# Attention with mixture-of-experts: raw w2 requested at the end of a step, and new w2 split ahead of scaling y and joining h

## The chip, the cores and the metric

The kernel runs on one core of one Trainium2 chip. The metric is the device time of one launch in microseconds (us). Engines are named as in the profile: PE (TensorE, matmuls), PEld (its weight loads), DVE (VectorE), ACT (ScalarE), POOL (GpSimd) and SP (SyncE), which issues DMAs. "SPq" and the like are the instruction queues of an engine.

## What is computed

A chunked attention is followed by a mixture of experts on its output.

```python
def reference(q, k, v, w_gate, w_local, w1, w2):   # q, k, v: (8, 8, 576, 64)
    # attention inside chunks of 64 tokens, per batch and head
    scores = (q_c @ k_c^T) / sqrt(64); attn = softmax(scores); out = attn @ v_c
    x = out.transpose(0, 2, 1, 3).reshape(8, 576, 512)
    # one expert per token: argmax of x @ w_gate, or the expert of the token before
    # where sigmoid(x @ w_local) >= 0.5
    h = relu(x[b, s] @ w1[e])                      # w1: (8, 512, 1024)
    out[b, s] = softmax(x @ w_gate)[e] * (h @ w2[e])   # w2: (8, 1024, 512)
```

There are 4608 tokens, 8 experts, and everything is float32.

## The kernel before

The attention comes first and writes x to DRAM. The tokens are then sorted by expert into tiles of at most 128 tokens, and the experts' part works on one tile after another. The change lies in this second part, in `step(t)` (lines 1053 to 1127), which runs for t = 3 to 40 here.

A matmul in full float32 is slow on PE, so the weights and the activations of a full tile are split into a rounded high part and the rest (hi and lo): `split` (line 104) makes `w2h` on ACT (line 105) and `w2l` on DVE (line 106) from `raw2`, in four chunks of 128x1024. One product is then three matmuls (hi hi, hi lo, lo hi). Every expert's remainder tile with at most 64 tokens is put first of its expert; such a *partial* tile is multiplied by the raw weights in plain float32 (`mm1_part`, line 664, and `mm2_part`, line 677, whose matmul is line 681), since the new weights aren't split yet. `kind[t]` says at run time whether tile t is partial, and every such choice is an If on registers.

Step t does, in program order:

- `mm1` of tile t (x times w1, into PSUM `h`), its softmax factor (`probs`, lines 644 to 651), and `planes` (line 723): ACT and DVE copy h into 16-bit planes `hw`.
- POOL gathers the rows of tile t + 2 from DRAM; PE transposes x of tile t + 1 (line 763) and ACT and DVE split it (`xp`, lines 751 and 752). `refill(0, t)` splits new w1 where the expert turns after tile t.
- SP issues two DMA transposes `ht<-hw` (`turn_planes`, line 730), if tile t is full.
- SP issues `reload(1, t - 2)`: raw w2 of the next expert, two loads of 1 MB, if `fetch[t - 2]` is set (lines 1025 to 1031; line 1027 is the If). Then `reload(0, t)`, the same for raw w1.
- PE multiplies h of tile t - 1 by w2 into PSUM `y`: `mm2` (line 674) or `mm2_part`.
- `down_y`: DVE scales y into `ysb` (line 816, or lines 707 to 710 for a partial tile), and POOL scatters ysb to the output (line 819).
- `h_parts`: for a full tile `join` (line 732) waits for ht, copies the turned halves into `hsb` (lines 736 and 737) and makes hi and lo of `hp` (lines 739 and 740). For a partial tile PE transposes hsb (line 780) and ACT and DVE copy it to `hf`.
- `refill(1, t - 1)`: ACT and DVE split new w2 where the expert turns after tile t - 1 (`turn[t - 1]`).

Each engine executes its own instructions in this order (a manual schedule); only semaphores tie the engines together. Steps from 36 on (`tail`) are written otherwise: there `refill(1, t - 1)` and `reload(1, t - 1)` already stand at the end. `y` and the two banks of `h` have one PSUM buffer each. SP's queue carries all weight loads and all transposes of h.

In the run profiled, the tiles 6, 9, 18, 21, 28 and 35 are partial, each the first of its expert; tile 27 is a full tile and the only one of its expert.

Of the kernel before, what the change touches and what calls it, by code (L numbers as in the profile page):

```python
# [33 lines left out]
EARLY = 3  # L34
NTILE = EARLY + (N + E * (P - 1)) // P
# [34 lines left out]
def tile_attention_then_moe(ctx: ExitStack, tc, q, k_in, v, wg, wl, w1, w2, out):  # L70
# [33 lines left out]
    def split(hi, lo, raw, lo_eng=None):  # L104
        nc.scalar.copy(hi, raw)
        (lo_eng or nc.vector).tensor_tensor(lo, raw, hi.bitcast(F32), ALU.subtract)
# [424 lines left out]
    for b in range(B):  # L531
        t, p = divmod(b * S, P)
# [99 lines left out]
    def probs(xg, hot):  # L632
        pr, atoms = prob_atoms(xg, hot)
        run(atoms[:-1])
        return pr, atoms[-1]
# [21 lines left out]
    def mm1(xs, hs, c):  # L657
        for n, (a, w) in enumerate(PASSES):
            for j in range(2):
                nc.tensor.matmul(hs[j], xs[a][:, c], W1[w][c][:, 512 * j:512 * j + 512],  # L660
                                 start=(c == 0 and n == 0), stop=(c == 3 and n == 2))


    def mm1_part(xf, hs, M):
        n = F * M // P
        for c in range(4):
            for j in range(P // M):
                nc.tensor.matmul(hs[0][M * j:M * j + M, 0:n], xf[:, c, 0:M], raw1[c][:, n * j:n * j + n],
                                 start=(c == 0), stop=(c == 3))
# [14 lines left out]
    def new_h():  # L684
        return [ps_s.tile([P, 512], F32, name=f"h{j}", tag=f"sc{j}") for j in range(2)], pc.tile([P, F + 32], F32, name="hsb", bufs=1)[:, 0:F]
# [4 lines left out]
    def either(kind, plain, partial, sizes=False):  # L690
        if kind is None:
            plain()
            return
        with tc.If(kind != 0) as cmp:  # L694
            if sizes:
                with tc.If(kind != 1) as small:
                    partial(P // 4)
                with small.Else():
                    partial(HT)
            else:  # L700
                partial()
        with cmp.Else():
            plain()
# [8 lines left out]
    def relu(hsb, hs):  # L712
        for j in range(2):
            nc.scalar.activation(hsb[:, 512 * j:512 * j + 512], hs[j], AF.Relu)

    def relu_part(hsb, hs, M):
        nc.scalar.activation(hsb[:, 0:F * M // P], hs[0][:, 0:F * M // P], AF.Relu)

    def new_planes():
        return (pa2.tile([P, 2, 2, 512], U16, name="hw", tag="xT", bufs=1),  # L720
                pa2.tile([P, 2, 2, 4, P], U16, name="ht", tag="pr"))

    def planes(hw, hs):
        for n in range(2):
            for j, eng in enumerate((nc.scalar, V)):
                evac(eng, hw[:, j, n], hs[j].bitcast(U16)[:, n::2])

    def turn_planes(hw, ht):
        for j in range(2):
            nc.sync.dma_start(ht[:, j].rearrange("p a n t -> p (a n) t"), hw[:, j].rearrange("p a f -> p (a f)"), transpose=True)  # L730
# [28 lines left out]
    def x_parts(xg, kind, late=False, own=False):  # L759
        xp = part("xp", "pT" if late else None)  # L760
        ps = trp().rearrange("p (n t) -> p n t", n=4)
        for n in range(4):
            nc.tensor.transpose(ps[:, n], xg[:, P * n:P * n + P], ident)
        xf = pc.tile([P, 4, HT], F32, name="xf", **own_tag("xf", own))
        either(kind and kind[1], lambda: split4(ps, xp), lambda: share(xf, ps[:, :, 0:HT]))
        return xp[:, 0], xp[:, 1], xf
# [167 lines left out]
    def gather_full(t):  # L934
        xgs[t] = gather(t, pc.tile([P, XR], F32, name="xg", bufs=4), x_d)
# [63 lines left out]
    def reg(row, t, hi, engines, why=None):  # L999
        return nc.values_load(regs[0:1, row, t:t + 1], min_val=0, max_val=hi, engines=engines,  # L1000
                              skip_runtime_bounds_check_because=why)
# [4 lines left out]
    def refill(which, t):  # L1006
        hi, lo, raw = ((w1h, w1l, raw1), (w2h, w2l, raw2))[which]
        with tc.If(turn[t] != 0):  # L1008
            for c in range(3 if which == 0 else 4):
                split(hi[c], lo[c], raw[c])  # L1010
            if which == 0:
                with when(kind[t + 1] and kind[t + 1][1] == 0):
                    split(hi[3], lo[3], raw[3])
# [11 lines left out]
    def reload(which, t):  # L1025
        dst, w, k = ((pair1, w1, 2 * P), (pair2, w2, 4 * P))[which]
        with tc.If(fetch[t] != 0):  # L1027
            en = reg(1, t + 1, E - 1, [ET.SP])
            for g in range(2):
                nc.sync.dma_start(  # L1030
                    dst[g], w[bass.ds(en, 1), k * g:k * g + k, :].rearrange("a (c p) f -> p (a c) f", p=P))

    TMIN = N // P
# [6 lines left out]
    @contextmanager  # L1040
    def when(v, otherwise=None):
        if v is None:
            yield
        else:
            with tc.If(v) as cmp:  # L1045
                yield
            if otherwise:
                with cmp.Else():
                    otherwise()
# [3 lines left out]
    def step(t):  # L1053
        tail = t >= TMIN
        if t < NTILE:
            hs, hsb = new_h()
            with when(ok[t]):
                either(kind[t] and kind[t][2], lambda: [mm1(xps[t], hs, c) for c in range(4)],
                       lambda M: mm1_part(xps[t][2], hs, M), True)
                prc[t], last = probs(xgs[t], ehot[:, t])  # L1060
                hw, ht = (None, None) if tail else new_planes()
                either(kind[t] and kind[t][1], lambda: (last(), relu(hsb, hs) if tail else planes(hw, hs)),
                       lambda M: (last(), relu_part(hsb, hs, M), split(w1h[3], w1l[3], raw1[3])), True)
                if tail and t + 1 < NTILE:
                    xps[t + 1] = x_parts(xgs[t + 1], kind[t + 1], t != LAST, t == LAST)
        if t + 2 < NTILE:
            with when(ok[t + 1]):
                gather_full(t + 2)
        if t + 1 < NTILE:
            next_x(t + 1)  # L1070
        if not tail:
            if kind[t] is None:
                turn_planes(hw, ht)
            else:
                with tc.If(kind[t][3] == 0):
                    turn_planes(hw, ht)
        if EARLY < t <= TMIN:
            reload(1, t - 2)
        if t + 1 < NTILE:
            reload(0, t)  # L1080
        if t + 2 < NTILE and t + 2 not in kind:
            kind[t + 2] = kind_of(t + 2)
        if t + 2 < NTILE:
            turns(t + 1)
        y = new_y()

        def down(cs):
            def plain():
                for c in cs:
                    mm2(hps[t - 1], y, c)  # L1090

            either(kind[t - 1] and kind[t - 1][2], plain,
                   lambda: mm2_part(hps[t - 1][0][2], y, range(2 * cs[0], 2 * cs[-1] + 2)))

        def down_y():
            keep = t == LAST
            ysb = new_ysb(t > LAST)
            with when(ok[t - 1], (lambda: V.memset(ysb, 0.0)) if keep else None):
                scale_y(ysb, y, prc[t - 1], kind[t - 1])
                if not keep:  # L1100
                    put_y(t - 1, ysb)
            if keep:
                kept.append((t - 1, ysb))

        if t < NTILE:
            hps[t], hp, hf = new_hp(tail and t != LAST, t == LAST)
        if tail and t < NTILE:
            cuts = ((0, 1, 2, 3),) if t == LAST else ((0, 1), (2, 3))
            with when(ok[t - 1]):
                down(cuts[0])  # L1110
            if t != LAST:
                with when(ok[t]):
                    h_parts(hsb, (0,), kind[t], hp, hf)
                with when(ok[t - 1]):
                    down(cuts[1])
            down_y()
            with when(ok[t]):
                h_parts(hsb, (1,) if t != LAST else (0, 1), kind[t], hp, hf)
            refill(1, t - 1)
            reload(1, t - 1)  # L1120
        else:
            with when(ok[t - 1]):
                down((0, 1, 2, 3))
            down_y()
            if t < NTILE:
                h_parts(hsb, (0, 1), kind[t], hp, hf, ht)
                refill(1, t - 1)

    def next_x(t):
        if EARLY < t <= TMIN:  # L1130
            xps[t] = x_parts(xgs[t], kind[t], t == TMIN)
        refill(0, t - 1)
# [44 lines left out]
```

## Time and profile before

| | us |
|---|---|
| median of two runs | 702.25 (700.42 to 704.07) |
| the profiled execution | 705.32 |
| its span, first to last instruction | 703.40 |
| PE busy in it | 622.7 |

The profile is of one execution of its own, and its times add up to 705.32, not to the median. A line of a timeline gives the start (us from the span's start), the duration, the engine, the source line, the operation, what it writes and reads, how many instructions were merged, and in brackets the idle time ahead of it and what ended that. The granted clock is a share of TensorE's full 2.4 GHz.

### The profile page before, as it was taken

What the parts mean: (1) busy time and instruction counts of PE and PEld (TensorE: products, weight loads), DVE (VectorE), ACT (ScalarE), POOL (GpSimd) and SP (SyncE); (2) the same over time, 40 slices, a digit from 0 to 9 for tenths busy, and PEclk for the clock granted to TensorE, in tenths of its full rate; (3) what the DMA queues carried; (4) which work ended last, traced back from release to release, by engine and by line L of the source; (5) the groups of instructions that cost most, each with busy time, mean ns of one, the idle gap of its engine ahead of it and who ended that gap; (6) DMA issues with size and microseconds to landing.
All of it is one profiled execution on the core that took longest, in us unless ns stands there. A gap on an engine that the chain in (4) does not pass through costs nothing. (4 is left out here: it accounts for less than half of the span.)

```text
span 703.4 us, 16455 instructions
## 1 busy us (share of the span) xinstructions
PE 622.7 (89%) x5458; PEld 487.4 (69%) x5458; DVE 408.2 (58%) x1008; ACT 308.8 (44%) x528; POOL 170.1 (24%) x286
## 2 busy tenths in 40 slices
PE   3899989779999968969999969889998699999993
PEld 3688867567778756648787646667876487877882
DVE  1566658675885775655555656744578445674331
ACT  2577756654313543523434444523456233453220
POOL 3334433672231211211212111212113112121101
PEclk9999999999999998989999989989999899999997
DMA  8999999987544443837554353629377385554201
GB/s 189 245 211 281 250 264 252 274 255 267 161 136 77 78 179 68 261 88 207 97 101 87 79 178 85 265 64 217 90 199 251 84 214 102 81 187 150 64 18 36
DMA packets 142318, 112.41 MB, mean 160 GB/s; under 512 B 99280, under 2 KB 118736, under 8 KB 142160
## 3 DMA queue, kind: packets, MB, share of 16 engines
q1 hardware_dynamic: 135520, 89.86, 51.7%
q0 software_dynamic: 6640, 20.65, 8.7%
q8 instruction: 75, 1.23, 0.7%
q14 instruction: 83, 0.68, 0.3%
HBM read 77.28 MB, written 20.35 MB: 139 GB/s over the span
## 5 line engine op out<-in xcount | busy, mean ns | idle before, releaser
L674 PE MATMUL y<-w2h,hp 128*128 128x512 f32 x560 | 186.3, 402 | 4.8 <-ACTq L1008 2.2
L660 PE MATMUL h<-w1h,xp 128*128 128x512 f32 x560 | 161.9, 398 | 0.0
L819 POOL DMA_INDIRECT out<-ysb,sidx x41 | 44.4, 1084 | 397.5 <-DVE ysb L816 274.1
L674 PEld LDWEIGHTS y<-w2h,hp 128*128 128x128 f32 x560 | 106.6, 190 | 27.5 <-ACTq L1008 2.7
L660 PEld LDWEIGHTS h<-w1h,xp 128*128 128x128 f32 x560 | 102.1, 188 | 20.0
L674 PE MATMUL y<-w2l,hp 128*128 128x512 f32 x280 | 110.9, 396 | 1.7 <-DVEq L1008 1.0
L660 PE MATMUL h<-w1l,xp 128*128 128x512 f32 x280 | 86.9, 391 | 0.0
L736 ACT COPY hsb<-ht 128x512 uint16<-128x512 uint16 x54 | 40.7, 772 | 92.3 <-DMA ht<-hw 86.7
L816 DVE TENSOR_SCALAR ysb<-y,ppr 128x512 f32<-128x512 f32 x35 | 26.3, 751 | 80.1 <-PE tr L802 45.1
L674 PEld LDWEIGHTS y<-w2l,hp 128*128 128x128 f32 x280 | 53.6, 191 | 13.5 <-DVEq L1008 2.2
L681 PE MATMUL y<-raw,hf 128*64 128x256 f32 x192 | 32.5, 510 | 33.9 <-SPq L1027 19.3
L660 PEld LDWEIGHTS h<-w1l,xp 128*128 128x128 f32 x280 | 52.5, 188 | 11.9 <-DVEq L1008 0.2
L179 PE MATMUL tr<-ident,qk 128*128 128x128 f32 x288 | 44.0, 301 | 14.1 <-POOL qk L171 6.4
L171 POOL COPY qk<-qk 128x512 f32<-128x512 f32 x69 | 40.1, 614 | 58.7 <-issue 26.3
L169 ACT COPY qkT<-tr 128x512 f32<-128x512 f32 x69 | 37.7, 589 | 30.1 <-PE tr L179 23.5
L681 PEld LDWEIGHTS y<-raw,hf 128*64 128x64 f32 x192 | 19.5, 188 | 45.2 <-issue 42.7
L179 PEld LDWEIGHTS tr<-ident,qk 128*128 128x128 f32 x288 | 34.9, 153 | 21.3 <-POOL qk L171 11.1
L739 ACT ACTIVATE hp<-hsb 128x512 fp32r<-128x512 f32 x54 | 31.0, 622 | 41.8 <-DVE hsb L737 40.0
L627 POOL DMA_INDIRECT xg<-x_d,gidx x39 | 44.6, 1143 | 15.1 <-issue 13.9
L646 ACT ACTIVATE pex<-pex 128x8 f32<-128x8 f32 x41 | 8.6, 210 | 84.3 <-DVE pex L645 84.3
L740 DVE SCALAR_TENSOR_TENSOR hp<-hsb,hp 128x512 fp32r<-128x512 f32 x54 | 35.0, 690 | 14.5 <-ACT hp L739 14.5
L171 DVE COPY hw<-h 128x512 uint16<-128x512 uint16 x54 | 34.8, 686 | 8.9 <-PE h L660 4.7
(220 smaller groups left out, 876.8 us busy)
## 6 DMA issues: line engine op xcount, KB each, us to landing
raw<-in_moe_w SPq DMA_DIRECT2D x28, 1024.0 KB, 6.5
raw<-in_moe_w SPq DMA_DIRECT2D x16, 512.0 KB, 5.6
qk<-in_q SPq DMA_DIRECT2D x11, 512.0 KB, 6.5
qk<-in_k SPq DMA_DIRECT2D x11, 512.0 KB, 7.0
v<-in_v SPq DMA_DIRECT2D x22, 256.0 KB, 6.0
x_d<-xs SPq DMA_DIRECT2D x7, 521.0 KB, 6.6
x_d<-x_w2h SPq DMA_DIRECT2D x6, 521.0 KB, 7.0
x_d<-x_w2l SPq DMA_DIRECT2D x5, 521.0 KB, 8.0
```

The lines of the kernel that those rows point to most:

```text
L169: eng.copy(dst, src)
L171: eng.tensor_copy(dst, src)
L179: nc.tensor.transpose(box["ps"][:, n], src_of(n), ident)
L627: nc.gpsimd.indirect_dma_start(out=dst, out_offset=None, in_=src, in_offset=bass.IndirectOffsetOnAxis(ap=gidx[t].bitcast(U32), axis=0))
L660: nc.tensor.matmul(hs[j], xs[a][:, c], W1[w][c][:, 512 * j:512 * j + 512], start=(c == 0 and n == 0), stop=(c == 3 and n == 2))
L674: nc.tensor.matmul(y, hx[f // 4][a][:, f % 4], W2[w][c][:, f % 2, :], start=(f == 0 and n == 0), stop=(f == 7 and n == 2))
L681: nc.tensor.matmul(y[HT * j:HT * j + HT, 0:n], hf[:, f % 4, HT * (f // 4):HT * (f // 4) + HT], raw2[f // 2][:, f % 2, n * j:n * j + n], st ...
L736: nc.scalar.copy(bits[:, j, :, :, 1], ht[:, j, 1])
L739: nc.scalar.activation(hp[j][:, 0], full[:, j], AF.Relu)
L740: V.scalar_tensor_tensor(hp[j][:, 1], full[:, j], 0.0, hp[j][:, 0].bitcast(F32), ALU.max, ALU.subtract)
L816: either(kind and kind[1], lambda: V.tensor_scalar(ysb, y, pr, None, ALU.mult), lambda: y_part(ysb, y, pr))
L819: nc.gpsimd.indirect_dma_start(out=out, out_offset=bass.IndirectOffsetOnAxis(ap=sidx[t].bitcast(U32), axis=0), in_=ysb, in_offset=None, bo ...
```

## The change

In steps below 36, raw w2 is no longer requested behind the transposes of step t for tile t - 2, but at the end of step t for tile t - 1, behind the w1 reload. And `refill(1, t - 1)`, the split of new w2, moves from the end of the step to right behind `mm2` of tile t - 1, ahead of the scaling of y and of `h_parts`.

```diff
@@ step(t)
                 with tc.If(kind[t][3] == 0):
                     turn_planes(hw, ht)
-        if EARLY < t <= TMIN:
-            reload(1, t - 2)
         if t + 1 < NTILE:
             reload(0, t)
...
         else:
             with when(ok[t - 1]):
                 down((0, 1, 2, 3))
+            if t < NTILE:
+                refill(1, t - 1)
             down_y()
             if t < NTILE:
                 h_parts(hsb, (0, 1), kind[t], hp, hf, ht)
-                refill(1, t - 1)
+                reload(1, t - 1)
```

SP's queue in step 5 before, from its transposes to the If of the w1 reload (raw_0_85 and raw_1_86 are raw w2, raw_0_83 and raw_1_84 raw w1, L1027 the If of a reload):

```order
L730 DMA_TRANSPOSE ht<-hw 128x8x128 x2
L1075 UNCONDITIONAL_BRANCH x2
L1027 COMPARE_AND_BRANCH
L1000 TENSOR_LOAD regs
L1000 ISA x2
L1030 ISA
L1030 DMA raw_0_85<-in_moe_w 128x4x512
L1030 ISA
L1030 DMA raw_1_86<-in_moe_w 128x4x512
L1027 UNCONDITIONAL_BRANCH x2
L694 UNCONDITIONAL_BRANCH
L1027 COMPARE_AND_BRANCH
```

In the changed kernel the transposes of step 5 are followed by the w1 reload at once; this is the end of that reload and what stands behind it, up to the branch at the end of the w2 reload:

```order
L1030 DMA raw_1_84<-in_moe_w 128x2x1024
L1027 UNCONDITIONAL_BRANCH x2
L1008 UNCONDITIONAL_BRANCH
L1000 TENSOR_LOAD regs x2
L1027 COMPARE_AND_BRANCH
L1000 TENSOR_LOAD regs
L1000 ISA x2
L1030 ISA
L1030 DMA raw_0_85<-in_moe_w 128x4x512
L1030 ISA
L1030 DMA raw_1_86<-in_moe_w 128x4x512
L1027 UNCONDITIONAL_BRANCH x2
```

The w2 reload has moved behind the w1 reload, and so out of the stretch between one step's transposes and the w2 matmuls of the same step. It stands ahead of the next step's transposes.

ACT's queue in step 5 before, from the join to the split of w2 (in brackets the semaphores that a row waits on: an engine's name, or DMAHW for the DMAs of SP):

```order
L736 COPY hsb<-ht 128x512 [waits DMAHW4_49,Activation_49]
L736 COPY hsb<-ht 128x512 [waits DMAHW5_49]
L739 ACTIVATE hp_4110<-hsb 128x512 [waits DVE_49,PE_49,Activation_49]
L739 ACTIVATE hp_4111<-hsb 128x512 [waits DVE_49,PE_49,Activation_49]
L694 UNCONDITIONAL_BRANCH
L1008 COMPARE_AND_BRANCH
L105 CAST w2h<-raw_0_85 128x1024 [waits DMAHW6_49,DMAHW3_49,Activation_49]
L105 CAST w2h<-raw_0_85 128x1024 [waits DMAHW7_49,Activation_49]
L105 CAST w2h<-raw_1_86 128x1024 [waits DMAHW7_49,DMAHW2_49,Activation_49]
L105 CAST w2h<-raw_1_86 128x1024 [waits DMAHW3_49,Activation_49]
```

The same place in the changed kernel, from the register loads at the head of the stretch to the first copy of hf:

```order
L1000 TENSOR_LOAD regs x2
L1008 COMPARE_AND_BRANCH
L105 CAST w2h<-raw_0_85 128x1024 [waits DMAHW4_49,DMAHW3_49,PE_49]
L105 CAST w2h<-raw_0_85 128x1024 [waits DMAHW7_49,PE_49]
L105 CAST w2h<-raw_1_86 128x1024 [waits DMAHW5_49,DMAHW2_49,PE_49]
L105 CAST w2h<-raw_1_86 128x1024 [waits DMAHW3_49,PE_49]
L1008 UNCONDITIONAL_BRANCH
L1008 UNCONDITIONAL_BRANCH [waits Activation_49]
L1027 UNCONDITIONAL_BRANCH
L694 COMPARE_AND_BRANCH
L696 COMPARE_AND_BRANCH
L169 COPY hf<-tr 128x2x2x32 [waits PE_49]
```

The four casts now stand ahead of hf and of the join, and each has a wait on PE of its own. On DVE the four subtractions (line 106) moved in the same way, ahead of the scaling of y.

PE's queue in step 5 before, at the w2 matmuls of a partial tile (line 681):

```order
L763 MATMUL tr<-ident,xg 128x128 x3
L694 UNCONDITIONAL_BRANCH x2
L1008 UNCONDITIONAL_BRANCH
L1075 UNCONDITIONAL_BRANCH
L1027 UNCONDITIONAL_BRANCH
L1000 TENSOR_LOAD regs
L694 COMPARE_AND_BRANCH
L681 MATMUL y<-raw_0_85,hf 64x256 [waits DMAHW4_49,DMAHW3_49,DMAHW6_49,DVE_49,Activation_49]
```

And in the changed kernel:

```order
L763 MATMUL tr<-ident,xg 128x128 [waits DMASW1_49]
L763 MATMUL tr<-ident,xg 128x128 x3
L1000 TENSOR_LOAD regs
L694 COMPARE_AND_BRANCH
L681 MATMUL y<-raw_0_85,hf 64x256 [waits DMAHW2_49,DMAHW3_49,DVE_49,DMAHW4_49,Activation_49]
```

The matmuls themselves don't move. They wait on DMA counters of SP in both; which counters these are has changed with SP's order.

## Rows read from the trace of the kernel before

**Rows 1.** Page, part 1: busy time, share, instructions of the engines

```profile
PE 622.7 (89%) x5458; PEld 487.4 (69%) x5458; DVE 408.2 (58%) x1008; ACT 308.8 (44%) x528; POOL 170.1 (24%) x286
```

**Rows 2.** Page, part 5: group, busy, mean ns | idle before, releaser

```profile
L681 PE MATMUL y<-raw,hf 128*64 128x256 f32 x192 | 32.5, 510 | 33.9 <-SPq L1027 19.3
```

**Rows 3.** Timeline of PE: line 681 at places 1 to 5, then the control

```profile
266.48 5.18 PE L681 MATMUL y<-raw,hf 128*64 128x256 f32 x32 [8.16 <-DMA ht<-hw]
...
306.49 5.64 PE L681 MATMUL y<-raw,hf 128*64 128x256 f32 x32 [6.86 <-SPq L1027]
...
418.55 5.93 PE L681 MATMUL y<-raw,hf 128*64 128x256 f32 x32 [6.46 <-DMA ht<-hw]
...
459.78 5.80 PE L681 MATMUL y<-raw,hf 128*64 128x256 f32 x32 [5.84 <-SPq L1027]
...
551.43 6.05 PE L681 MATMUL y<-raw,hf 128*64 128x256 f32 x32 [6.56 <-SPq L1027]
...
632.13 1.95 PE L681 MATMUL y<-raw,hf 128*64 128x256 f32 x16
```

**Rows 4.** Stretches: us; PE, PEld, DVE, ACT, POOL busy (count); clock, DMA, GB/s

```profile
258.00:266.50 8.50, 0.34 (x5) 0.14 (x3) 6.09 (x13) 3.04 (x6) 0.00 (x0) 0.78 0.67 193
266.50:272.00 5.50, 5.50 (x34) 3.50 (x35) 0.79 (x2) 1.53 (x2) 0.00 (x0) 0.72 0.14 31
...
634.00:637.00 3.00, 3.00 (x27) 2.00 (x26) 1.54 (x3) 1.26 (x3) 0.00 (x0) 1.00 0.05 11
```

**Rows 5.** Timeline of all engines around place 1 (tile 6 partial)

```profile
252.78 1.25 SPq L1030 DMA_DIRECT2D raw<-in_moe_w  x2
254.02 0.75 DVE L816 TENSOR_SCALAR ysb<-y,ppr 128x512 f32<-128x512 f32 x1 [1.52 <-issue]
...
255.31 0.29 DVE L171 COPY hf<-tr 128x128 f32<-128x128 f32 x1 [0.33 <-ACT hf L169]
255.37 3.89 ACT L105 CAST w2h<-raw 128x1024 fp32r<-128x1024 f32 x4
...
256.46 4.63 DVE L106 TENSOR_TENSOR w2l<-raw,w2h 128x1024 fp32r<-128x1024 f32 x4 [0.86 <-ACT w2h L105]
...
263.02 2.66 SPq L730 DMA_TRANSPOSE ht<-hw  x2
264.05 0.68 DVE L752 TENSOR_TENSOR xp<-tr,xp 128x512 fp32r<-128x512 f32 x1
```

**Rows 6.** Timeline of DVE and PE at place 5's turn (tile 27 full)

```profile
521.86 3.49 DVE L106 TENSOR_TENSOR w1l<-raw,w1h 128x1024 fp32r<-128x1024 f32 x3
526.76 0.75 DVE L816 TENSOR_SCALAR ysb<-y,ppr 128x512 f32<-128x512 f32 x1 [1.40 <-PE h L668]
...
528.65 1.29 DVE L740 SCALAR_TENSOR_TENSOR hp<-hsb,hp 128x512 fp32r<-128x512 f32 x2 [0.44 <-ACT hp L739]
...
530.13 0.49 PE L674 MATMUL y<-w2h,hp 128*128 128x512 f32 x1 [1.40 <-ACT w2h L105]
...
538.34 0.60 PE L780 MATMUL tr<-ident,hsb 128*128 128x128 f32 x4
```

**Rows 7.** SP: w2 load, next transposes; landings of both, and transposes without load (278.60)

```profile
323.38 1.19 SPq L1030 DMA_DIRECT2D raw<-in_moe_w  x2
330.84 4.54 SPq L730 DMA_TRANSPOSE ht<-hw  x2
...
DMA to landing us min/median/max: 5.6/8.6/11.6
...
DMA to landing us min/median/max: 5.2/5.5/5.8
...
DMA to landing us min/median/max: 3.1/3.1/3.2
```

**Rows 8.** Timeline behind place 1: join of tile 8, then its w2 matmuls

```profile
283.20 1.38 ACT L736 COPY hsb<-ht 128x512 uint16<-128x512 uint16 x2 [1.61 <-issue]
...
287.12 0.50 PE L674 MATMUL y<-w2h,hp 128*128 128x512 f32 x1
```

## Prediction, made before the changed kernel was run

> **What bounds the kernel now.** I read the page first, then TensorE's waits and timeline, then the stretches with their granted clock, and last all engines around one stall. PE is busy for 89% of the span [rows 1], so the end is set by PE's stream and by the holes in it. Among the costly groups one has a hole of its own: the matmuls of a small tile against raw w2 (line 681), with 33.9 us of idle time in front of 32.5 us of work [rows 2]. The timeline [rows 3] shows where the 33.9 us lie: five stalls of 8.16, 6.86, 6.46, 5.84 and 6.56 us (sum 33.88), each ahead of the 32 matmuls of one partial tile. I call them places 1 to 5; the partial tiles are 6, 9, 18, 21 and 28.
>
> What ends such a stall? The profile names SP's branch at line 1027 three times and the landing of ht twice. Line 1027 is the If around the reload. The matmuls of line 681 wait on DMA counters (the order's rows in the section on the change show it), and since a branch of SP releases them, SP must advance them also where it skips the load. In a step of before that If stands behind the two transposes of the same step. At place 1 the transposes were issued from 263.02 to 265.68 and PE went on at 266.48, though hf had been ready since 255.60 and raw w2 had been in use by ACT since 255.37 [rows 5]. So PE waits for SP to pass a skipped branch, and SP waits for the planes of the next tile, which wait behind the split of w2 (ACT to 259.26, DVE to 261.09). A control lies in the same trace: the sixth partial tile is multiplied in step 36, where the code already has the reload last. There the first half of line 681 starts with no idle before it [rows 3].
>
> The stall costs a second time. In the stretch around it the granted clock is 0.78, and 0.72 in the 5.5 us behind it, a mix of 1.2 and 2.4 GHz; at the control it is 1.00 [rows 4]. The 32 matmuls take 5.18, 5.64, 5.93, 5.80 and 6.05 us at the five places, 28.60 together; at the control 16 take 1.95, so 32 take 3.90 [rows 3]. At full clock five would take 19.50: another 9.10 us.
>
> **Part 1, the reload at the end of the step.** Line 681 of tile t' (in step t'+1) now depends on a branch that SP passes at the end of step t', behind the w1 reload, and not behind the transposes of step t'+1. At place 1 that w1 reload was issued at 252.78 to 254.03 [rows 5], over 4 us before PE is ready. So the whole 33.88 + 9.10 = 42.98 us is open, and the question is what is late next. Nothing is added: as many instructions, and the two 1 MB loads are the same.
>
> **Part 2, the split first.** In the five turn steps the splits (ACT 3.89, DVE 4.63 us [rows 5]) come ahead of scaling y and of hf. ACT may start a chunk as soon as PE has done with it, since each cast has its own wait on PE. From the end of DVE's split to the last hf it takes what it took before: 254.02 to 255.60, 1.58.
> - Place 1: before its row at 254.02 DVE stood idle for 1.52 us without any wait that the profile shows, so I let it start there. It now splits to 258.65, and the last hf ends about 260.3. PE is ready at 258.32 (266.48 less 8.16), so 2.1 us of the 8.16 stay. Whether 2.1 us of idle still costs clock is open; I take 4.5 us for the 32 matmuls, between 3.9 and 5.18, so line 681 ends about 264.9. DVE then has probs, planes and xp: 261.09 to 264.73 before, some 0.7 us earlier now. mm1(8) starts at 265.0 instead of 271.7 (266.48 + 5.18): gain 6.7.
> - Places 2, 3 and 4, by the same chain: the last hf is done before or as PE gets there, since PE ran mm2 longer after DVE's xp. The gain is the stall and the slow clock, less about 0.1: 6.86 + 1.74, 6.46 + 2.03, 5.84 + 1.90, so 24.5 together.
> - Place 5 is the one turn whose next tile (27) is full, so here the split stands ahead of a join. DVE ends its w1 split at 525.35 and started scaling at 526.76 [rows 6]. Now it splits w2 in between, 4.63 us, and scales from 531.5; the first hp follows 1.89 us behind the scaling's start, as before (526.76 to 528.65). So mm2(27) starts about 533.4, not 530.13. Before, it began with a wait of 1.40 us for w2 and took 8.2 us to 538.34 [rows 6]; I take 7.9 now (weights ready, but a slow start behind a hole of some 4 us), so it ends 3.0 later. Its own stall behind is 6.56 + 2.15 = 8.71, so net 5.7. In steps that turn no weights the split is a skipped branch and costs nothing that PE sees.
>
> **What is late next.** The 2 MB of raw w2 are now requested ahead of the next step's transposes in SP's queue instead of behind them. The nearest rows: loads at 323.38, transposes at 330.84, 7.5 us later. The second half of the load landed 11.6 us after its issue, the transposes 5.2 and 5.8 us after theirs, against 3.1 where no load was under way [rows 7]. That is 2 to 3 us late. After places 2, 4 and 5 a full tile follows, whose whole mm1 hides it. After places 1 and 3 the next tile is partial again; there join starts at 283.20 and mm2 at 287.12, hard on its heels [rows 8], though ACT alone holds join back by 1.61 us. The bounds are 0 and 2.7 us each (5.8 less 3.1); I take 1.2, 2.4 for both.
>
> **The sum.** 6.7 + 24.5 + 5.7 - 2.4 = 34.5 us. The profiled execution took 705.32 us (span 703.40), so 670.8; the runs' median is 702.25, 3.07 less, so **668 us**. With no clock lost in small holes (place 1 at 3.9 us, mm2 of place 5 at 6.0) and ht at 0 it is 663; with 5.18 at place 1, a mm2 of 8.9 at place 5 and ht at 2.7 each, 673.
>
> **A rule that speaks against it.** On the row above transposes behind a load land 2 to 3 us late. The Trainium skill, "DMA: Bandwidth & Descriptors", section "Queues, rings and completion order", says that on each DMA engine descriptors are consumed in ring order, and SP owns one ring per engine. By that rule a transpose starts only when the load ahead of it is drained; the trace agrees in direction (5.2 against 3.1 us). What it would give at its worst is the last rival below.
>
> **Rivals.**
> - The clock stays low. The holes left (2.1 us at place 1, some 4 at place 5, some tenths elsewhere) keep PE at half clock in line 681. For: at place 5 a wait of 1.40 us went with a mm2 of 8.2 us, and behind a stall 0.72 is granted [rows 4, 6]. Against: the control. Then what was counted of the 9.10 falls away (0.68 at place 1, 5.67 at 2 to 4, 2.15 at 5: 8.5), and 26.0 are left: **676 us**.
> - The landing of ht is what PE waits for at places 1 and 3, as the profile says there. Then only 6.86 + 5.84 + 6.56 go, with 5.79 of clock, less 3.0 and 2.4: 19.7, about **683 us**. Against: the first transpose was issued at 263.02 and landings take 3.1 to 5.8 us, so the landing can fall beside SP's passing by chance; places 2, 4 and 5 have the same code.
> - It doesn't do what it says: SP reaches the earlier branch no sooner, because the w1 reload ahead of it waits for the w1 split. Then about **702 us**. Against: at place 1 SP issued that w1 load at 252.78, and PE was ready at 258.32.
> - Slower: SP's queue holds the transposes behind the w2 load until its last byte. The load's second half landed 11.6 us after its issue, 12.4 after the first half's (323.38, issues some 0.8 apart: 1.19 for both, 0.4 each); transposes 7.5 us behind would start 4.9 late and then take 5.8, so land 7.6 later than 3.1. Here the gap is about 1 us shorter, an estimate: 8.6. If no mm1 hid that and every such hole cost 1.8 us of clock (9.10 over five), five places cost 5 x 10.4 = 52: **720 us**. It decides from about 7 us a place, where the 34.5 are gone. Against: at 330.84 the delay was 2.7 at most, and no stall of PE came of it.
>
> **How the numbers follow.** Chances: forecast (662 to 674) 0.58, clock stays low 0.25, ht 0.07, no effect 0.05, slower 0.05. The low end 657 is the open 42.98 us nearly whole (705.32 - 42.98 - 3.07 = 659) with 2 us for the spread of the runs; the high end 685 takes in the ht rival. Within 2% of 702.25 (688.2 to 716.3), about what a measurement of this kernel can tell from no change, lie the case without effect and part of the last one. So faster 0.90, same 0.07, slower 0.03.
>
> **What would show it.** In the profile after: no line-681 row with more than some 2 us of idle ahead of it except perhaps at place 1, 32 of its matmuls in 4 to 4.5 us, granted clock near 1.00 around them, SP's loads of w2 ahead of the transposes; mm2 of tile 27 starting later by some 3 us; ht landings of 5 to 6 us behind each w2 load. It is wrong if line 681 still waits 5 us or more, or if ACT's wait for ht grows into a PE stall in the steps behind places 1 to 5.

## The result, and the profile after

The changed kernel took **677.01 us** (median of two runs, 676.41 to 677.62) against 702.25: a ratio of 0.964, 95% interval 0.953 to 0.976. Beside other variants it was timed twice more, at 675.21 and 673.71 us, the latter at 0.954 (0.950 to 0.958) of the kernel before. A median here is of all runs of a batch, while a ratio leaves out slow runs, those more than 1.5% above the kernel's fastest (four of six in the batch of 675.21 us, where the other two took 671.32 and 664.72). It is faster, by some 4%, and the forecast of 668 was 9 us too low. The profiled execution took 677.62 us, with a span of 675.5.

Page, part 1 of the kernel after; it answers to [rows 1]:

```profile
PE 621.7 (92%) x5458; PEld 485.2 (72%) x5458; DVE 407.8 (60%) x1008; ACT 307.6 (46%) x528; POOL 167.5 (25%) x286
```

PE has the same work, 1 us less of it, in a span that is 28 us shorter. The groups of PE after (busy us, mean ns | idle us ahead, and what ended it), answering to [rows 2]:

```profile
L674 PE MATMUL y<-w2h,hp 128*128 128x512 f32 x560 | 187.2, 404 | 8.9 <-ACT hp L739 7.7 <-ACTq L1045 1.2
...
L681 PE MATMUL y<-raw,hf 128*64 128x256 f32 x192 | 22.3, 382 | 1.6 <-ACT hf L169 1.6
L668 PE MATMUL h<-raw,xf 128*32 128x256 f32 (+1 forms) x144 | 19.3, 491 | 5.6 <-issue 3.9 <-ACTq L1008 1.8
```

The 33.9 us ahead of line 681 are 1.6 now, and its 192 matmuls take 22.3 us instead of 32.5. But two other groups wait longer. Before, they stood like this (kernel before, same view):

```profile
L674 PE MATMUL y<-w2h,hp 128*128 128x512 f32 x560 | 186.3, 402 | 4.8 <-ACTq L1008 2.2 <-ACT w2h L105 1.4 <-ACTq L1045 1.2
...
L668 PE MATMUL h<-raw,xf 128*32 128x256 f32 (+1 forms) x144 | 16.8, 453 | 3.0 <-ACT hsb L736 2.8 <-PE tr L802 0.2
```

Line 668 is `mm1_part`, the first matmul of a partial tile against raw w1. PE's timeline after shows where it waits; two of the five line-681 rows that answer to [rows 3] stand with it (the other three, at 300.46, 441.17 and 525.90, also have no idle ahead and take 3.67):

```profile
264.89 3.67 PE L681 MATMUL y<-raw,hf 128*64 128x256 f32 x32 [1.63 <-ACT hf L169]
...
282.78 1.93 PE L668 MATMUL h<-raw,xf 128*32 128x256 f32 x32 [1.78 <-ACTq L1008]
...
286.78 0.50 PE L674 MATMUL y<-w2h,hp 128*128 128x512 f32 x1 [1.48 <-ACT hp L739]
...
402.28 3.67 PE L681 MATMUL y<-raw,hf 128*64 128x256 f32 x32
...
422.63 6.15 PE L668 MATMUL h<-raw,xf 128*64 128x512 f32 x16 [3.85 <-issue]
...
511.61 0.79 PE L674 MATMUL y<-w2h,hp 128*128 128x512 f32 x1 [3.92 <-ACT hp L739]
```

Behind place 1 line 668 of tile 9 waits 1.78 and mm2 of tile 8 1.48 us; behind place 3 line 668 of tile 21 waits 3.85; and mm2 of tile 27 waits 3.92. Stretches of the kernel after around place 1 and around the wait of 3.85 us (columns as in [rows 4]):

```profile
261.20:264.90 3.70, 2.07 (x13) 1.54 (x12) 3.37 (x6) 0.27 (x1) 0.33 (x1) 1.00 0.92 374
264.90:268.60 3.70, 3.70 (x33) 2.66 (x33) 3.08 (x11) 1.77 (x4) 1.66 (x2) 1.00 0.35 122
...
418.70:422.60 3.90, 0.08 (x1) 0.00 (x0) 2.18 (x3) 0.26 (x1) 0.00 (x0) 0.78 1.12 270
422.60:428.70 6.10, 6.07 (x16) 1.83 (x16) 3.74 (x11) 2.74 (x5) 2.13 (x2) 0.58 0.45 126
```

The clock is at 1.00 around line 681 now; the slow stretch has moved to line 668 of tile 21, at 0.58.

Where the time went is best counted from the first mm1 matmul of one full tile to that of another (the starts of line 660):

| from mm1 of tile to tile | before, us | after, us | gain |
|---|---|---|---|
| 7 to 8, place 1 | 19.56 | 12.56 | 7.00 |
| 8 to 10, over tile 9 | 21.79 | 25.36 | -3.57 |
| 10 to 11, place 2 | 18.69 | 9.80 | 8.89 |
| 17 to 19 | 23.39 | 21.57 | 1.82 |
| 19 to 20, place 3 | 18.58 | 9.90 | 8.68 |
| 20 to 22, over tile 21 | 23.24 | 29.03 | -5.79 |
| 22 to 23, place 4 | 17.85 | 9.81 | 8.04 |
| 27 to 29, w2 of tile 27 | 26.20 | 28.08 | -1.88 |
| 29 to 30, place 5 | 18.81 | 9.80 | 9.01 |
| 3 to 40, all (the rest 0.37) | 467.63 | 435.06 | 32.57 |

The part ahead of tile 3, which the change doesn't touch, took 206.28 before and 210.91 after: 4.6 us more. Over all the profiles of this study this start lies between 199.6 and 211.9 with the same work ahead of it, and in the changed kernel's two other profiles it is 206.41 and 207.82. So it is chance, and I compare the stretch from tile 3 to tile 40 (below: *the expert part*) beside the runs' medians. In the two other profiles of the changed kernel the expert part is 433.29 and 435.17. The rows behind places 1 and 3 are -2.64 and -4.13 in the first of them and -2.26 and -5.58 in the second, and from tile 12 to 13, behind place 2, both lose some 1.9 us that the profile above does not lose (13.69 and 13.55 against 11.74).

### The profile page after: what moved, and what is told of

It reads as the page before. It is cut to its first block, busy times and chain, and to the rows that moved or that the text cites. A ratio compares the mean times of both kernels' runs of the same rounds, so it can differ in the third digit from the quotient of the medians.

```text
span 675.5 us, 16457 instructions
## 1 busy us (share of the span) xinstructions
PE 621.7 (92%) x5458; PEld 485.2 (72%) x5458; DVE 407.8 (60%) x1008; ACT 307.6 (46%) x528; POOL 167.5 (25%) x286
## 5 line engine op out<-in xcount | busy, mean ns | idle before, releaser
L179 PEld LDWEIGHTS tr<-ident,qk 128*128 128x128 f32 x288 | 35.8, 156 | 21.5 <-issue 10.1
L627 POOL DMA_INDIRECT xg<-x_d,gidx x39 | 42.7, 1094 | 14.9 <-issue 9.7
L169 ACT COPY hw<-h 128x512 uint16<-128x512 uint16 x54 | 29.0, 589 | 22.3 <-PE h L660 18.9
L106 DVE TENSOR_TENSOR w2l<-raw,w2h 128x1024 fp32r<-128x1024 f32 x28 | 32.4, 1220 | 8.6 <-ACT w2h L105 8.6
L227 DVE TENSOR_REDUCE mx<-sc 128x8 f32<-128x512 f32 x36 | 23.2, 686 | 21.8 <-PE sc L216 21.8
```

What stands on the lines that cost most here:

```text
L169: eng.copy(dst, src)
L179: nc.tensor.transpose(box["ps"][:, n], src_of(n), ident)
L227: nc.vector.tensor_reduce(mxs[a], sc[a // 8].rearrange("p h c k -> p (h c) k"), AX.X, ALU.max)
L627: nc.gpsimd.indirect_dma_start(out=dst, out_offset=None, in_=src, in_offset=bass.IndirectOffsetOnAxis(ap=gidx[t].bitcast(U32), axis=0))
```

## What SP did behind the places

The timeline of SP after, behind places 1 and 3: the w2 load (line 1030) and the next two transposes (line 730).

```profile
272.69 1.19 SPq L1030 DMA_DIRECT2D raw<-in_moe_w  x2
278.10 4.00 SPq L730 DMA_TRANSPOSE ht<-hw  x2
...
412.19 1.35 SPq L1030 DMA_DIRECT2D raw<-in_moe_w  x2
415.98 5.97 SPq L730 DMA_TRANSPOSE ht<-hw  x2
```

The load goes out only 5.4 and 3.8 us ahead of the transposes. Two transposes are otherwise issued in some 2.6 us (263.02 in [rows 5]); here it takes 4.00 and 5.97, and by the tile's view of ht they land 5.3 and 7.0 us after issue. What stands behind them in SP's queue gets late too: the If of the w1 reload, which line 668 of the next, partial tile waits for. So theory A is: the w2 load holds up the transposes, these make `join` late and hold the w1 If, and the first waits ahead of mm2 and the second ahead of line 668. The rivals: the new waits come from the order of the splits, or PE waits for something else in those steps. The letters in the expectations below are those of each text.

## Experiments: the two parts of the change apart

**The reload alone.** Only the w2 request at the end of the step; the split stays behind the join.

```diff
-        if EARLY < t <= TMIN:
-            reload(1, t - 2)
...
                 refill(1, t - 1)
+                reload(1, t - 1)
```

> Only the reload moves to the end of the step; the split of w2 stays behind the join. Theory A (PE waited for SP to pass the reload's branch): line 681 loses its five stalls here too. Then DVE, which does hf first and the split after, is late with xp: the stretches from mm1 of the full tile behind a partial one to the next mm1 come out at 12.7, 10.9, 10.9, 10.1 and 10.8 us instead of the 12.6, 9.8, 9.9, 9.8, 9.8 of the changed kernel, and the turn to tile 27 keeps its 26.2 us instead of 28.1. Together 677 to 680 us. Theory B (the split's place made the gain, because planes and transposes come sooner): line 681 keeps stalls of 5 us and more and the time stays at 698 to 703.

Measured: 696.19 us, ratio 0.985 (0.981 to 0.990); expert part 460.1. Neither number came. Line 681 is free of waits as theory A has it (0.0 us idle in its group), but mm2 waits elsewhere. PE's timeline of this kernel:

```profile
325.47 0.66 PE L674 MATMUL y<-w2h,hp 128*128 128x512 f32 x1 [4.32 <-ACTq L1008]
```

There are three large waits of this kind (4.32, 4.45 and 3.50 us) and smaller ones (1.41, 1.30 and 0.71); one of 1.81 ahead of mm2 of tile 27 is for the split itself. Line 668 waits 2.88 and 4.27. Line 1008 is the If around a split: PE waits for ACT to pass the If of `refill`, which stands behind the join. SP's timeline in the same step:

```profile
309.57 1.18 SPq L1030 DMA_DIRECT2D raw<-in_moe_w  x2
311.74 6.97 SPq L730 DMA_TRANSPOSE ht<-hw  x2
```

The load is only 2.2 us ahead of the transposes here, and they take 6.97 us to issue. It is so late because it may overwrite raw w2 only when ACT and DVE have passed the If of the split in that step, which stands behind the join, although nothing is split there: the profile has SP's load waiting 2.2 us for DVE's last `hp` of the join (line 740), which ends at 309.31.

**The split alone**, with the reload where it was.

```diff
                 down((0, 1, 2, 3))
+            if t < NTILE:
+                refill(1, t - 1)
             down_y()
...
-                refill(1, t - 1)
```

> Only the split of w2 moves ahead of the scaling and the join; the w2 reload stays behind the transposes of the step. Theory A: the five stalls of line 681 stay, each ended by SP, shorter by less than 1 us, and the turn to tile 27 costs 2 us more: 699 to 704 us. Theory B: the gain is here, 675 to 685 us.

Measured: 700.35 us, ratio 0.993 (0.990 to 0.997); expert part 462.4. Line 681 keeps 29.5 of its 33.9 us of idle. So the parts are worth some 7.5 and 5.3 us of expert part alone and 32.6 together (467.6 less 460.1, 462.4 and 435.1). They need each other: the reload's place frees line 681, and the place of the split's If lets the load out earlier, further ahead of the next transposes.

**The w1 If ahead of the transposes**, on top of the change:

```diff
+        if t + 1 < NTILE:
+            reload(0, t)
         if not tail:
             ...
-        if t + 1 < NTILE:
-            reload(0, t)
```

> The changed kernel with the w1 reload ahead of the step's transposes in SP's queue. Theory C (the new waits of 1.78 and 3.85 us ahead of the raw w1 matmuls of tiles 9 and 21 are for SP to pass the w1 reload's branch behind transposes that a w2 load holds up): both go below 0.3 us; behind place 1 the landing of ht still decides, so little comes of it there, behind place 3 some 3 us and the slow clock (16 matmuls in 6.15 us) are gained; the transposes of tile 26 come 3 to 4 us later. 672 to 676 us. Theory D (they wait for ACT or DVE, which the profile names at the first): the waits stay and the time is that of the changed kernel within 1 us.

Measured: 681.21 us, ratio 0.964 (0.958 to 0.969); expert part 443.4, so 8 more than the change. What it tells apart it told: line 668 has 0.0 us of idle now, so the wait there is for the w1 If in SP's queue. Behind place 1 nothing is won by that: mm2 of tile 8 now waits 3.21 us, as long as line 668 and mm2 waited together (1.78 + 1.48 = 3.26). And the loads of w1 now stand ahead of the transposes as well, and mm2 pays. PE's timeline:

```profile
501.36 0.79 PE L674 MATMUL y<-w2h,hp 128*128 128x512 f32 x1 [8.16 <-ACT hp L739]
```

That is tile 26, behind a w1 load. The expected gain was a miss.

## Experiments: size, time and queue of the load

**Half of each w2 load**, on top of the change (`range(2 - which)` in `reload`).

> The change with only the first 1 MB of each w2 reload (the second half of raw w2 keeps the weights of an expert before: this part of the computation is left out). Theory A (the load holds up the transposes behind it): with half the bytes the transposes of tiles 8 and 20 are issued in under 3.2 us, the waits ahead of line 668 at tiles 9 and 21 fall from 1.78 and 3.85 us to under 0.7 and 2, and the time is 667 to 672 us. Theory C (not the load, but the order of splits, joins and branches): the waits stay and the time is 675 to 679.

Measured: 667.14 us, ratio 0.945 (0.939 to 0.951); expert part 429.5. SP's timeline behind place 1, and line 668's group:

```profile
273.88 0.42 SPq L1030 DMA_DIRECT2D raw<-in_moe_w  x1
279.11 2.76 SPq L730 DMA_TRANSPOSE ht<-hw  x2
```
```profile
L668 PE MATMUL h<-raw,xf 128*32 128x256 f32 (+1 forms) x144 | 16.8, 454 | 1.7 <-SPq L1027 0.9 <-DMA ht<-hw 0.8
```

With half the bytes and about the same 5.2 us between them the transposes are not stretched. The waits of line 668 fall to 0.81 and 0.88 us. The stretches over tiles 9 and 21 take 23.75 and 24.43 us, so of the 9.36 us lost there 6.2 are back (3.6 and 4.7 against the other two profiles of the change). The wait of mm2 of tile 27 stays (3.73), so that one isn't the load's.

Nor is the wait of mm2 of tile 8 behind place 1, where theory A is wrong. It grows from 1.48 to 2.46 us, as much as line 668 waits less (0.81 + 2.46 = 3.27 against 3.26). In both kernels mm2 starts 8.68 us behind its tile's first transpose, and in the kernel before it was 8.52 (287.12 in [rows 8] less 278.60). ACT's part of `hp` waits for DVE's copy of hsb, which comes behind the w1 split and the scaling of y. Timelines of the change, then of the half load:

```profile
286.10 1.15 ACT L739 ACTIVATE hp<-hsb 128x512 fp32r<-128x512 f32 x2 [1.03 <-DVE hsb L737]
```
```profile
287.11 1.15 ACT L739 ACTIVATE hp<-hsb 128x512 fp32r<-128x512 f32 x2 [1.69 <-DVE hsb L737]
287.79 0.50 PE L674 MATMUL y<-w2h,hp 128*128 128x512 f32 x1 [2.46 <-ACT hp L739]
```

So behind place 1 the load decides how long line 668 waits, but not when mm2 goes on. Behind place 3, where 3.85 us become 0.88 and 0.53 ahead of mm2, the load decides.

**The same half in the kernel with the reload alone.**

> The reload at the end of the step with the split behind the join, as in the run of the first part alone (696.2 us), and only the first 1 MB of each w2 reload (the second half is left out of the computation). Theory A (there the load comes out only 2 us ahead of the transposes, so their issue takes 6.9 us instead of 2.7, and mm2 waits 3.5 to 4.5 us for join): with half the bytes those four waits fall below 2 us and the time is 681 to 688. Theory C (join is late because of what ACT and DVE do ahead of it): the waits stay, 693 to 698.

Measured: 671.37 us, ratio 0.951 (0.946 to 0.956); expert part 438.6. Theory A held and was too careful: the waits of 3.5 to 4.5 us fall below 0.7, and 21.5 us come back (460.1 less 438.6). The split's place is thus worth 25.0 us with the whole load (460.1 to 435.1) and 9.1 with half of it (438.6 to 429.5): most of its worth, 15.9 us, is that it lets the load out in time.

**The load in another queue**: the w2 reload issued by GpSimd at the same place.

```diff
-        with tc.If(fetch[t] != 0):
-            en = reg(1, t + 1, E - 1, [ET.SP])
+        eng, at = ((nc.sync, ET.SP), (nc.gpsimd, ET.Pool))[which]
+        with tc.If(sub(fetch[t], [at]) != 0):
+            en = reg(1, t + 1, E - 1, [at])
             for g in range(2):
-                nc.sync.dma_start(
+                eng.dma_start(
```

> The change with the w2 reload issued by GpSimd at the same place of the step, so in another queue than the transposes. Theory A1 (it is the order within SP's queue that holds up the transposes): each transpose is issued in about 1.3 us and lands in 3 to 4, no wait ahead of line 668 above 0.7 us, and the time is 666 to 671. Theory A2 (the DMA engines are shared, whichever queue asked): issues stay at 2 us or more each, landings at 5 or more, the waits ahead of line 668 and of mm2 stay, 674 to 679. Theory D (GpSimd issues the load late or slowly, behind gathers and scatters): the splits of the next turn or line 681 wait again, 680 or more.

Measured: 675.22 us, ratio 0.957 (0.950 to 0.963); expert part 441.8. Timelines of POOL and SP behind places 1 and 3:

```profile
263.26 1.64 POOL L1031 DMA_DIRECT2D raw<-in_moe_w  x2 [0.37 <-issue]
268.24 4.54 SPq L730 DMA_TRANSPOSE ht<-hw  x2
...
403.27 1.61 POOL L1031 DMA_DIRECT2D raw<-in_moe_w  x2 [0.29 <-ACT hsb L736]
406.94 6.36 SPq L730 DMA_TRANSPOSE ht<-hw  x2
```

The transposes are held up all the same, and line 668 waits 2.20 and 4.11 us. So it is not the order inside SP's queue; theory A2 is what is left: something that both queues share, by that theory the DMA engines. The expert part is 6.7 us longer than the change's. Of the 5.2 us in line 681's group 3.5 are for GpSimd's loads, as theory D said in small, and behind place 4 mm2 of tile 23 waits 1.98 us for `hp`, in a stretch (tile 24 to 25) of 15.84 us instead of 11.73. The profiled execution (671.97 us) hides this behind a short start (201.15 us to tile 3).

**When the transposes get out.** Each row of this table is one w2 load and the transposes behind it, from the SP and POOL timelines (t is counted from the load's first issue):

| kernel, place | load to transposes, us | issue of both, us | last issue ends at t |
|---|---|---|---|
| reload alone, 1 | 1.91 | 6.86 | 8.8 |
| reload alone, 311.74 | 2.17 | 6.97 | 9.1 |
| POOL's queue, 3 | 3.67 | 6.36 | 10.0 |
| after, 3 | 3.79 | 5.97 | 9.8 |
| POOL's queue, 1 | 4.98 | 4.54 | 9.5 |
| after, 1 | 5.41 | 4.00 | 9.4 |
| registers behind, 1 (below) | 6.54 | 2.77 | 9.3 |
| reload alone, half the load, 1 | 1.87 | 4.08 | 6.0 |
| half the load, 1 | 5.23 | 2.76 | 8.0 |

Whatever the queue, behind 2 MB the second transpose of these rows is through SP 9 to 10 us after the load was asked for, behind 1 MB at 6.0. Over places 1 to 4 of the eight profiles with such a load of 2 MB at the end of the step, it is 8.4 to 10.4 us for the 27 pairs up to 5.6 us behind the load. The distance alone doesn't decide: 6.54 us behind the load a pair took its plain 2.8, but at place 4 in the two later profiles of the change pairs 6.28 and 6.17 us behind took 4.58 and 4.71, and the pair of [rows 7], 7.46 us behind, 4.54.

The landing fits better. By the views of raw's landings, the second half landed 8.1 us after its own issue at place 1 with POOL's queue: issued at 264.1, so landed at 272.2, where the transposes' issue ended at 272.78. The same fits [rows 7]: 11.6 us there, landing at about 335.8, and the transposes' issue ends at 330.84 + 4.54 = 335.38. In all nine pairs for which a trace has this landing, the issue ends between 0.5 us ahead of it and 0.9 behind it. The transposes get through about when the load's last bytes land.

## Experiments: a version that beats the change

**Register loads behind the load.** In the step's middle every engine loads registers for the steps ahead (`kind_of`, `turns`); on SP two of these loads stand between the transposes and the w2 load. This variant moves them to the end of the step:

```diff
             reload(0, t)
-        if t + 2 < NTILE and t + 2 not in kind:
-            kind[t + 2] = kind_of(t + 2)
-        if t + 2 < NTILE:
-            turns(t + 1)
...
                 reload(1, t - 1)
+        if t + 2 < NTILE and t + 2 not in kind:
+            kind[t + 2] = kind_of(t + 2)
+        if t + 2 < NTILE:
+            turns(t + 1)
```

> Theory A (the w2 load is requested only 5.4 and 3.8 us ahead of the next transposes in SP's queue and holds them up, and behind them the branch of the w1 reload): with SP's register loads for the steps ahead moved behind the w2 load, the load is issued 1.4 to 2.7 us sooner, the two transposes of tiles 8 and 20 are issued in 3 to 3.5 us instead of 4.0 and more, the waits ahead of line 668 at tiles 9 and 21 fall from 1.78 and 3.85 us to under 1 and 2.5, and the time is 671 to 675 us. Theory C (the new waits come from the order of the splits, not from the load): nothing changes, 675 to 679.

Measured: 665.45 us, ratio 0.942 (0.936 to 0.948); expert part 431.8. SP's timeline behind place 1, then PE's:

```profile
260.83 1.18 SPq L1030 DMA_DIRECT2D raw<-in_moe_w  x2
267.37 2.77 SPq L730 DMA_TRANSPOSE ht<-hw  x2
```
```profile
270.82 1.93 PE L668 MATMUL h<-raw,xf 128*32 128x256 f32 x32 [0.69 <-ACTq L1008]
...
409.12 3.65 PE L668 MATMUL h<-raw,xf 128*64 128x512 f32 x16 [2.62 <-issue]
```

The waits fell to 0.69 and 2.62 us, close to what theory A gave. The load comes 2.1 us behind the transposes' end instead of 2.7: 0.6 sooner, not 1.4. As the start was short too (200.44), it was run a second time, with the change beside it.

> The changed kernel beside the variant with the register loads moved. Theory A (that variant's gain is the shorter hold of the transposes, about 3 us in the expert part): change 673 to 678 us. Rival (its 665 us was the share of the attention part that comes out shorter by chance): both within 2 us of each other.

> The change with the register loads behind the w2 load, a second time. Theory A: 2 to 6 us under the change, ratio to before near 0.945 to 0.955; from the first mm1 of tile 3 to that of tile 40 about 432 us against 434. Rival: no difference beyond 2 us.

Measured: the change 673.71 us, ratio 0.954 (0.950 to 0.958), expert part 435.2; the variant **669.01 us**, ratio 0.947 (0.943 to 0.951), expert part 431.3. So it beats both kernels, by 3.9 us over the change in the expert part and 4.7 in the median; the intervals of the two ratios just overlap, but each of its two profiles has a shorter expert part than each of the change's three (431.8 and 431.3, against 435.1, 433.3 and 435.2). In its second profile the load was 4.28 and 5.27 us ahead at places 1 and 3, and line 668 waited 2.53 and 2.50 us. The rival (no difference beyond 2 us) fell, though how much of the 4 us is the load's distance and how much the register loads of the other engines was not told apart.

**The split by kind**, on top of that: in front where the step's own tile is partial, behind the join where it is full.

```diff
-                refill(1, t - 1)
+                refill(1, t - 1, kind[t] and kind[t][1] != 0)
             down_y()
...
                 h_parts(hsb, (0, 1), kind[t], hp, hf, ht)
+                if kind[t]:
+                    refill(1, t - 1, kind[t][1] == 0)
```

> As the run before, and the split of w2 stands in front only in steps whose own tile is partial; in the step of a full tile it stands behind the join, as in the kernel before. Theory A (the wait of some 4 us ahead of mm2 of tile 27 is the split of 4.63 us that stands ahead of that tile's join): this wait falls to about 1.4 us as before, the other waits stay, and the time is 1 to 3 us under the run before. Rival (the wait has another cause, the transposes of tile 27 landing late): it stays at 4 us, and so does the time.

Measured: 696.07 us, ratio 0.986 (0.982 to 0.991); expert part 459.9. PE's timeline:

```profile
326.98 0.79 PE L674 MATMUL y<-w2h,hp 128*128 128x512 f32 x1 [4.09 <-ACTq L1008]
...
525.23 0.50 PE L674 MATMUL y<-w2h,hp 128*128 128x512 f32 x1 [1.82 <-ACT w2h L105]
```

The wait ahead of mm2 of tile 27 fell from 4.11 to 1.82, so theory A is right on that: there the split is what stands ahead of the join. Its time was a bad miss, and an instructive one. At 326.98 nothing is split behind the join, the second If is skipped; but it stands there, and both the w2 load and PE wait until ACT and DVE have passed it. It is the wait of the reload alone (4.32 at the same place) and has its cause: the If that is skipped, not the work in it. What the extra If in every step costs by itself was not told apart. SP's timeline in the kernel with the split by kind, behind place 1:

```profile
275.18 1.18 SPq L1030 DMA_DIRECT2D raw<-in_moe_w  x2
277.86 5.71 SPq L730 DMA_TRANSPOSE ht<-hw  x2
```

The load is 2.7 us ahead of the transposes again, and line 668 waits 3.64 us there.

## Why the prediction was right, and where it was off

- *What bounds the kernel.* Right. With the If passed a step earlier line 681 has 1.6 us of idle in all. The split alone left 29.5 and the reload alone 0.0, so it is the reload's place. The rival "the landing of ht is what PE waits for" fell with that, and "it doesn't do what it says" too.
- *Place 1.* Forecast gain 6.7 with 2.1 us of wait left; measured 7.00 with 1.63 (7.4 in the two other profiles). DVE's split runs first, as worked out, and hf follows 1.5 us behind its end (timeline of DVE after):

```profile
259.00 4.63 DVE L106 TENSOR_TENSOR w2l<-raw,w2h 128x1024 fp32r<-128x1024 f32 x4 [1.58 <-ACT w2h L105]
263.55 0.74 DVE L816 TENSOR_SCALAR ysb<-y,ppr 128x512 f32<-128x512 f32 x1
...
264.83 0.29 DVE L171 COPY hf<-tr 128x128 f32<-128x128 f32 x1 [0.33 <-ACT hf L169]
```

- *Places 2 to 4.* Forecast 24.5, measured 8.89 + 8.68 + 8.04 = 25.6. The 32 matmuls take 3.67 us at full clock, less than the 3.90 doubled from the control. "The clock stays low" fell for line 681. That its 676 us lie nearer to the measured 677 than the forecast does is chance.
- *Place 5.* Forecast 5.7 net: the stall gives 8.71, the turn to tile 27 takes 3.0. Measured 9.01 and 1.88, so 7.1; the hole "of some 4 us" ahead of mm2 of tile 27 is 3.92.
- *What is late next.* **This step failed**: the term "I take 1.2, 2.4 for both". It measured 3.57 + 5.79 = 9.36 us behind places 1 and 3, and 6.8 and 7.8 in the two other profiles. In those two a full tile's mm1 doesn't hide it behind place 2 either: mm2 of tile 11 waits 1.42 and 1.30 us for `hp`. Three things were missed. First, the distance: the row 7.5 us apart in [rows 7] was taken as the measure, and the last rival made it "about 1 us shorter". It is 5.4 and 3.8, because the load waits for its place in the queue behind the step's transposes, the w1 If and register loads, and the next step is short. Second, only ht was thought late. The w1 If stands behind the transposes, and line 668 waits on it just as line 681 waited on the w2 If: the wait of places 1 to 5 in another place, 1.78 and 3.85 us, the second with clock lost behind it (16 matmuls in 6.15 us; with 0.88 us of wait they took 3.65). Third, behind place 1 part of the loss is not the load's at all: mm2 of tile 8 waits for DVE's part of the join, with half the load too.
- *The slower rival* had the better mechanism: transposes get through about when the load's last bytes land. Its price was too high, since the load was through after 9 to 10 us and not 12.4, and since a full tile's mm1 hides most of it behind places 2, 4 and 5. And the reason isn't that queue: the load in POOL's held them up as much. So the rule of the Trainium skill on ring order ("DMA: Bandwidth & Descriptors", section "Queues, rings and completion order") gives the right sign, but is not what these runs show to decide.
- *The sum.* Forecast 34.5, measured 32.57 in the expert part: +0.3 at place 1, +1.1 at 2 to 4, +1.4 at 5, -7.0 for what is late next, +2.2 that the sum didn't have. It is only 1.9 us off because these misses cancel, which is luck. Of the last term 1.82 lie between tiles 17 and 19. There the forecast's "costs nothing that PE sees" holds for a skipped split in front, but before, it did cost: mm2 of tile 17 waited 1.30 and 0.32 us for ACT and DVE to pass the skipped If behind the join, and PE went on at a granted clock of 0.79; after, it waits 1.42 us for `hp` and goes on at 1.00. PE's timeline and the stretch behind the wait before, then after:

```profile
398.00 0.50 PE L674 MATMUL y<-w2h,hp 128*128 128x512 f32 x1 [1.30 <-ACTq L1008]
398.82 0.50 PE L674 MATMUL y<-w2l,hp 128*128 128x512 f32 x1 [0.32 <-DVEq L1008]
...
398.00:406.00 8.00, 7.68 (x27) 5.94 (x27) 3.75 (x11) 2.12 (x4) 1.45 (x1) 0.79 0.40 127
```
```profile
390.14 0.50 PE L674 MATMUL y<-w2h,hp 128*128 128x512 f32 x1 [1.42 <-ACT hp L739]
...
390.10:396.10 6.00, 5.96 (x25) 4.59 (x26) 4.24 (x11) 3.76 (x7) 1.86 (x2) 1.00 0.29 91
```

  Between tiles 17 and 19 the profiles of before, of the reload alone and of that with half the load, all with the If behind the join, take 23.35 to 23.39 us; those with the If in front take 20.47 to 21.57. The split by kind, which has it behind the join there but loads registers later, takes 21.33 (it waits 0.85 us, and the clock stays at 1.00). So most of the 1.82 us is clock, and why 1.42 us of waiting cost none is open.
- *The rest of the miss* between 668 and 677 is not the change's: 4.6 us by which the start was longer in this profile, and the 3.07 taken off for the median of before, where the median of after lies only 0.6 under its profile. In the batch where both were run side by side most often the gain is 704.89 less 673.71 = 31.2 us.

## What to carry to other kernels

An If that is skipped still has to be passed: whoever waits for what it guards waits for all that stands ahead of it in that engine's queue, so look for every consumer of such an If, the ones that were not late before above all. When a load is moved ahead of something urgent in time, work out the distance between them in the shortest step and compare it with how long the load takes to land. Two edits can be worth two and a half times as much together as the two added up (32.6 against 12.8 us here), and only running each alone shows that.

## What the runs showed of the hardware

- The issue of a DMA transpose itself gets longer while a large load is under way: two take 2.6 to 2.8 us alone and 3.7 to 7.0 up to 5.6 us behind the request of a 2 MB load, and they end 8.4 to 10.4 us after the request, about when the load's last bytes land, whether the load is in SP's or in GpSimd's queue. How the engines share this inside was not tried.
- The clock after a hole: its length alone doesn't tell whether clock is lost. After 1.63 us of idle line 681 still ran at 1.00. Ahead of tile 21's 16 matmuls of line 668, 2.62 us of idle cost none in the first profile of the variant with the register loads moved (3.65 us, at 1.00), 2.50 us did in its second (5.03 us, at 0.72), and 3.85 us in the changed kernel cost more (6.15 us, at 0.58). So holes well under those of before ([rows 3]) can cost clock, and need not.
